# Spectral layer, rational layer and expert layer on one core: loads, buffers and weight work moved at the borders between the layers

## The chip, the cores and the metric

The kernel runs on one core of one Trainium2 chip, as one launch. The metric is the device time of that core in microseconds. A core has five engines that each work through a queue of their own: TensorE (PE; its weight loads are shown apart as PEld), VectorE (DVE), ScalarE (ACT), GpSimd (POOL) and SyncE (SP). Sixteen DMA engines move data. SyncE and GpSimd issue the transfers here.

## The reference

The reference is a chain of three layers on `x` of shape (8, 3072, 256), in float32:

```python
X = np.fft.rfft(x, axis=1)
Yr = soft(X.real @ w_r - X.imag @ w_i + b_r)     # soft: sign(v) * max(|v| - 0.01, 0)
Yi = soft(X.real @ w_i + X.imag @ w_r + b_i)
x = np.fft.irfft(Yr + 1j * Yi, n=3072, axis=1).reshape(8 * 3072, 256)

h = x @ w_in                                     # 256 -> 2048
g = (a0 + a1 h + a2 h^2 + a3 h^3) / (1 + |b0||h| + |b1| h^2 + 1e-6)
x = g @ w_out                                    # 2048 -> 256

expert_idx = argmax(norm(x) @ norm(expert_emb).T / tau)     # 8 experts, top 1
gate_w = softmax weight of the chosen expert
out[mask_e] = gate_w * (relu(x[mask_e] @ w1[e]) @ w2[e])    # 256 -> 1024 -> 256
```

There are 24,576 tokens.

## The kernel before

Float32 products are done as three products of rounded parts: each operand is split into a high part (cast by ScalarE) and a low part (the rest, subtracted by VectorE or GpSimd), and high times high, high times low and low times high are summed in PSUM.

**Spectral layer** (`dft_phase`). Each of 8 batches goes through a DFT in two stages, a product with the weights for each of 13 groups of frequencies, and the inverse. For a group, GpSimd makes low parts (`m_low`, tile `yl`, L358, and `ys_low`, tile `ysl`, L369), TensorE runs the first inverse stage into `pu` and `pt`, and SyncE stores the result `u` to a buffer `ub` in device memory (L393 to L398). When all of a batch's groups are stored, six loads (`su_load`, L406) bring `ub` back as `su`, and the last inverse stage follows. Of the last batch this last stage is left to the rational layer (`ai`, L1072). The tasks carry dependencies, a step number and a duration from a table, and `list_order` writes out from them the order in which each engine gets its instructions. In idle places of this phase the rational layer's weights are split as well (`weight_steps`, 32 pieces, stored to `w_hl`, one piece each 2.85 steps). Its last tasks are five loads of 1 MB on GpSimd's queue, `next_area` (functions in `early`: `load_in` with the first weights, three `load_w`, one `load_x`; L849, L852), for the rational layer: its first weight matrix `wi` in four parts and the first tokens `xt0`.

**Rational layer** (`moe1_phase`). 768 steps of 128 hidden units by 512 tokens: `pe_h` (h, L1001), ScalarE's powers (`act_hb`, L1010, into `hb`, whose two buffers lie in the tile `d_outer_b`), VectorE's denominator, GpSimd's and VectorE's numerator, `pe_o` (L1063) with the second weights `wo`. The tables `LATENCY`, `SLOWER`, `SHIFT` and `COST` and `list_order` fix the order on every engine. Four loads of 1 MB bring `wo` in (`load_wo`, L957), and one load per two token tiles brings `xt` (`load_xt`, L960). The twelve pieces of `ai` stand between the first steps; each leads to a cast `ai_h` (L1082) and a difference `ai_l` (L1088) in two pairs of buffers that lie in the tile `l`, and to stores of both. Near its end the phase sorts the tokens by expert: GpSimd scatters the rows from two buffers to `xs` in device memory (L1175); one buffer lies in the tile `su`, the other in the tile `b`, and the four scatters from `b` come last.

**Expert layer** (`moe2_phase`). Fifty slots run, each of one expert. A slot has 512 tokens, two of them (40 and 49) have 256. `load(s)` issues on SyncE the rows `xr` (L1383) and the expert's weights `w1` and `w2` (L1390, L1391) into the right-hand memory area. `prep(s)` gives closures: transposes of the rows (`xpose`, L1461, with an identity matrix `ident`), the splits of four pieces of W1 and four of W2 (`wsplit`: L1467 a cast in two instructions, L1468 the low parts), and the gate's small VectorE chain (`guess`, `newton`, `root`, and so on). `products` (L1502) runs TensorE: for f = 0 to 7 six matmuls into `ph` (three PSUM buffers in turn, L1510), each followed by ScalarE's `hh` (L1515) and VectorE's `hl` (L1516); then for each part `a` of 128 tokens 24 matmuls into `py` (L1527), the scaling `y` on ScalarE (L1533) and a scatter on GpSimd (L1534). In between it issues the closures of the next slot:

```python
for q in nxt[8 // parts * a:8 // parts * (a + 1)]:   # after py of part a, before its y
    for t in q:
        t()
```

In a full slot there are four parts, and the last takes `[W2[0], newton]` and `[W2[1], root]` of the next slot; in a half slot there are two, and the last takes `W1[2]`, `W1[3]`, `W2[0]` and `W2[1]` with their gate steps. W2[2] and W2[3] follow beside the next slot's `ph`.

**Memory.** `Area` keeps a stretch of on-chip memory that all three layers use, from the right: `d_outer` (`l`, `b`, `su`, `fd`, in this order), under it the spectral layer's or the rational layer's own part (`wi0`, `wi1`, `xt`), and in the expert layer `e_area` in their place. Tiles of a later area that lie over those of an earlier one wait for the last use of what lay there. With the old order of `e_area` the first rows `xr0` lie over `b`.

## Time and profile before

| | us |
|---|---|
| median of three runs | 4298.53 |
| the runs | 4296.80, 4304.39, 4298.53 |
| the profiled execution's own time | 4303.15 |
| its span in the trace | 4301.4 |
| TensorE busy | 4148.8 (96%) |
| VectorE busy | 3541.8 (82%) |
| ScalarE busy | 3196.1 (74%) |
| GpSimd busy | 2558.4 (59%) |

The profile's page gives busy time by engine and, in 40 slices of the span, the busy share of each engine, the clock that was granted to TensorE and what the DMA engines did. In this trace the spectral layer ends at 785.2 us, the rational layer's last matmuls are near 3112 us, and the expert layer's first product begins at 3128.5 us. A row of the timeline gives the start and duration of an instruction or of a run of like instructions, and in brackets how long the engine had stood idle before it and what ended the idle time. A row of the list of waits sums such idle time by what ended it.

### The profile page before, as it was taken

The page shows a single profiled execution, that of the slowest core. Times are in us where ns is not written, and L with a number is a line of the kernel's source. Part 1 is how long each engine was busy: PE and PEld are TensorE (multiplying, and loading weights), DVE is VectorE, ACT ScalarE, POOL GpSimd, SP SyncE. Part 2 cuts the span into 40 slices and gives each one's busy share as a digit, 9 for nine tenths or more (in the row PEclk, how much of TensorE's full clock was granted, in tenths as well). Part 3 has the DMA queues.
Part 4 walks back from the last instruction along what each step waited for, and adds up shares of the span by engine and source line. Part 5 has one row for each costly group of instructions (what it writes and reads, how often), then busy time and mean ns, then how long its engine had stood idle before and what let it go on. Part 6 is the DMA issues. An engine that isn't in the chain of part 4 may idle for free. (4 is left out here: it accounts for less than half of the span.)

```text
span 4301.4 us, 85375 instructions
## 1 busy us (share of the span) xinstructions
PE 4148.8 (96%) x31348; PEld 3952.6 (92%) x31348; DVE 3541.8 (82%) x7005; ACT 3196.1 (74%) x5889; POOL 2558.4 (59%) x2404
## 2 busy tenths in 40 slices
PE   7899989799999999999999999999889999999998
PEld 5788878799999999999999999999879999999988
DVE  6989888699999999999999999999866666666666
ACT  4555555699999999999999999999655555555555
POOL 2334334488889888988898889988811111111111
PEclk9999999899999999999999999999999999999999
DMA  7678876600001110100110011101044443444443
GB/s 257 227 260 270 303 258 210 222 27 35 33 30 37 40 34 30 45 31 33 33 43 32 33 40 35 34 31 41 28 171 134 136 145 135 135 135 136 147 136 125
DMA packets 226460, 458.88 MB, mean 107 GB/s; under 512 B 19428, under 2 KB 140764, under 8 KB 218581
## 3 DMA queue, kind: packets, MB, share of 16 engines
q1 hardware_dynamic: 198884, 342.37, 23.9%
q0 software_dynamic: 26688, 110.66, 7.4%
q8 instruction: 259, 4.24, 0.4%
q14 instruction: 197, 1.61, 0.1%
q10 hardware_dynamic: 432, 0.00, 0.0%
HBM read 286.98 MB, written 166.49 MB: 105 GB/s over the span
## 5 line engine op out<-in xcount | busy, mean ns | idle before, releaser
L1042 POOL TENSOR_TENSOR qg<-Q,gh 128x512 f32<-128x512 f32 x768 | 980.4, 1296 | 126.4 <-DVE gh L1038 119.1
L1063 PE MATMUL po<-gh,wo 128*128 128x256 f32 x6144 | 992.7, 284 | 0.2 <-DVE gh L1038 0.2
L1053 POOL TENSOR_TENSOR gl<-pr,r 128x512 fp32r<-128x512 f32 x672 | 861.6, 1298 | 77.6 <-ACT r L1034 36.1
L1063 PEld LDWEIGHTS po<-gh,wo 128*128 128x128 f32 x6144 | 837.4, 189 | 0.5 <-DVE gh L1038 0.5
L1534 POOL DMA_INDIRECT out_dram<-y,ids x196 | 204.7, 1044 | 970.3 <-ACT y L1533 578.7
L1063 PE MATMUL po<-gl,wo 128*128 128x256 f32 x3072 | 616.2, 282 | 8.2 <-POOL spacer L1174 5.4
L1001 PE MATMUL h<-m_area_xt,m_area_wi 128*128 128x256 f32 x4608 | 614.0, 285 | 8.2 <-DMA m_area_wi<-w_hl 5.9
L1016 DVE SCALAR_TENSOR_TENSOR Q<-h,d_outer_b 128x512 f32<-128x512 f32 x768 | 525.6, 684 | 89.8 <-ACT h L1013 85.0
L1001 PE MATMUL h<-xt,m_area_wi 128*128 128x256 f32 x4608 | 594.4, 280 | 0.2 <-DVE pr L1046 0.2
L1001 PEld LDWEIGHTS h<-m_area_xt,m_area_wi 128*128 128x128 f32 x4608 | 577.0, 191 | 9.4 <-DMA m_area_wi<-w_hl 6.7
L1038 DVE SCALAR_TENSOR_TENSOR gh<-h,r 128x512 fp32r<-128x512 f32 x768 | 506.5, 684 | 69.8 <-ACT r L1034 69.0
L1001 PEld LDWEIGHTS h<-xt,m_area_wi 128*128 128x128 f32 x4608 | 559.9, 188 | 0.4 <-DVE pr L1046 0.4
L1010 ACT ACTIVATE d_outer_b<-h 128x512 f32<-128x512 f32 x768 | 461.5, 601 | 126.4 <-PE h L1001 120.7
L1013 ACT ACTIVATE h<-h 128x512 f32<-128x512 f32 x768 | 462.7, 602 | 29.3 <-DVE Q L1016 29.2
L1063 PEld LDWEIGHTS po<-gl,wo 128*128 128x128 f32 x3072 | 473.7, 189 | 8.8 <-POOL spacer L1174 5.8
L1046 DVE SCALAR_TENSOR_TENSOR pr<-h,qg 128x512 f32<-128x512 f32 x672 | 457.8, 683 | 16.9 <-POOL qg L1042 16.7
L1510 PE MATMUL ph<-e_area_x,w1h 128*128 128x512 f32 (+1 forms) x1600 | 441.7, 392 | 12.6 <-DVE hl L1516 7.2
L1527 PE MATMUL py<-w2h,hh 128*128 128x256 f32 x1568 | 442.0, 282 | 0.0
L1527 PE MATMUL py<-w2h,hl 128*128 128x256 f32 x1568 | 438.3, 280 | 1.0 <-DVE hl L1516 1.0
L1527 PE MATMUL py<-w2l,hh 128*128 128x256 f32 x1568 | 438.7, 280 | 0.0
L1515 ACT ACTIVATE hh<-ph 128x512 fp32r<-128x512 f32 (+1 forms) x400 | 235.7, 589 | 266.2 <-PE ph L1510 266.0
L1031 ACT ACTIVATE r<-Q 128x1024 f32<-128x1024 f32 x384 | 406.9, 1060 | 5.8 <-DVE Q L1016 5.8
(276 smaller groups left out, 8723.1 us busy)
## 6 DMA issues: line engine op xcount, KB each, us to landing
e_area_w<-in_moe_w_dram SPq DMA_DIRECT2D x104, 1024.0 KB, 5.5
xt_hl<-o SPq DMA_DIRECT2D x84, 512.0 KB, 4.4
ab<-d_inner_a SPq DMA_DIRECT2D x48, 512.0 KB, 5.8
d_outer_su<-ub SPq DMA_DIRECT2D x48, 512.0 KB, 8.0
m_area_xt<-xt_hl POOLq DMA_DIRECT2D x24, 1024.0 KB
xt<-xt_hl POOLq DMA_DIRECT2D x24, 1024.0 KB, 5.3
d_outer_l<-ab SPq DMA_DIRECT2D x96, 240.0 KB, 4.1
e_area_xr<-xs SPq DMA_DIRECT2D x40, 544.0 KB, 5.2
```

Source lines behind the costliest of these rows:

```text
L1001: nc.tensor.matmul(p[:, TT * e:TT * e + TT], lhsT=w[:, k, c0:c0 + 128], rhs=q[:, hl, k, :], start=(e == 0 and i == 0), stop=(i == 5), skip ...
L1010: nc.scalar.activation(sb("hb", s), sb("h", s), AF.Abs, scale=c.r_b0)
L1013: nc.scalar.activation(sb("h2", s), sb("h", s), AF.Square, scale=c.r_sb1)
L1016: V.scalar_tensor_tensor(out=pair("Q", s), in0=sb("h2", s), scalar=1.0 + 1e-6, in1=sb("hb", s), op0=ALU.add, op1=ALU.add)
L1031: nc.scalar.activation(sb("r0", s), sb("Q", s), AF.Abs_reciprocal_sqrt)
L1038: V.scalar_tensor_tensor(out=sb("gh", s), in0=sb("h", s), scalar=1.0 if fast else a0, in1=pair("r0", s), op0=ALU.add, op1=ALU.mult)
L1042: nc.gpsimd.tensor_tensor(out=sb("qg", s), in0=pair("Q", s), in1=sb("gh", s).bitcast(F32), op=ALU.mult)
L1046: V.scalar_tensor_tensor(out=h if kind(s) == "V" else sb("pr", s), in0=h, scalar=1.0 if fast else a0, in1=sb("qg", s), op0=ALU.add, op1=AL ...
L1053: nc.gpsimd.tensor_tensor(out=sb("gl", s), in0=sb("pr", s), in1=pair("r0", s), op=ALU.mult)
L1063: nc.tensor.matmul(po[:, TT * d:TT * d + TT], lhsT=w[:, p, 128 * d:128 * d + 128], rhs=v[:, TT * e:TT * e + TT], start=(f + e + i + d == 0 ...
L1510: nc.tensor.matmul(p, lhsT=w[:, k, 128 * f:128 * f + 128], rhs=v[:, k, :n], start=(i == 0), stop=(i == 5))
L1527: nc.tensor.matmul(p, lhsT=h[:, cols], rhs=w[:, f, :], start=(f == 0 and i == 0), stop=(f == 7 and i == 2))
```

## The change

It has six parts. (1) The tiles of `d_outer` and of `e_area` are laid in another order: `xr0` now lies over `l` and `fd`, `w10` over `l` and the area under it, and `w20`, `w11`, `x0` and `x1` over `su`. (2) The five early loads no longer depend on the previous batch's last store and are spread over the last batch, one behind each second group; the weight pieces are spaced by 2.7 steps. (3) Each `wo` load has a small copy ahead of it on GpSimd that reads what `act_hb` of step 1, 2, 3 or 4 wrote, and the first `xt` load stands behind `pool_q` of step 2; in the table `SLOWER` the entry from `load_wo` to `pe_o` goes from 5000 to 6000. (4) No identity matrix is made; the transposes read another one that stands in `c.rt`. (5) In front of the first slot six of the eight groups of closures run, and the last two (W2[0], W2[1] and their gate steps) go to f = 2 and 3 of that slot. (6) In `products` the closures of the last part come behind its `y` and its scatter.

```diff
-    outer = area.open("d_outer", l=([128, 8, 256], F32), b=([128, NG * 4 * GK], F32), su=([128, R2, 256], F32),
-                      fd=([R1, R1], F32))
+    outer = area.open("d_outer", l=([128, 8, 256], F32), fd=([R1, R1], F32), b=([128, NG * 4 * GK], F32),
+                      su=([128, R2, 256], F32))
...
-        task(next_area, i, "pool", 1038, [("next_area", i - 1)] if i else
-             [("a_store", (nb - 1, 5)), ("a_mm", (nb - 1, 11)), ("o_store", (nb - 2, 11))] + last, step=-1000)
+        task(next_area, i, "pool", 1038, [("next_area", i - 1), ("b_mm", (nb - 1, 2 + 2 * i))] if i else
+             [("a_store", (nb - 1, 5)), ("a_mm", (nb - 1, 11))] + last, step=-1000)
...
-        s = 5 + 2.85 * n
+        s = 5 + 2.7 * n
...
     def load_wo(i):
         f = slice(4 * i, 4 * i + 4)
+
+        nc.gpsimd.tensor_copy(spacer, sb("hb", i + 1)[:, 0:1])
         nc.gpsimd.dma_start(out=wo[:, f], in_=w_hl[1].rearrange("p (f h d) -> p f h d", h=2, d=256)[:, f])
...
-            task(load_wo, i, "pool", "dma", [], [("load_wo", i - 1)] if i else [], step=-1000)
+            task(load_wo, i, "pool", "dma", [("act_hb", i + 1)], [("load_wo", i - 1)] if i else [], step=-1000)
...
-                task(load_xt, tt // 2 + 1, "pool", "dma", last("pe_h"), step=s)
+                task(load_xt, tt // 2 + 1, "pool", "dma", last("pe_h") if tt else [("pool_q", 2)], step=s)
...
-    t = area.open("e_area", **{f"w1{i}": ([128, 2, 1024], F32) for i in range(2)},
-                   **{f"w2{i}": ([128, 8, 256], F32) for i in range(2)},
-                   **{f"xr{i}": ([128, 4, ROW], F32) for i in range(4)},
-                   **{f"x{i}": ([128, 2, 512], F32R) for i in range(4)})
+    shapes = {"w1": ([128, 2, 1024], F32), "w2": ([128, 8, 256], F32), "xr": ([128, 4, ROW], F32),
+              "x": ([128, 2, 512], F32R)}
+    t = area.open("e_area", **{nm: shapes[nm[:-1]] for nm in ("x3", "w10", "xr0", "w21", "xr2", "xr3", "x2", "xr1", "x0", "x1",
+                                                              "w11", "w20")})
...
-                nc.tensor.transpose(p[:, 128 * a:128 * a + 128], xr[:, a, o:o + 128], ident)
+                nc.tensor.transpose(p[:, 128 * a:128 * a + 128], xr[:, a, o:o + 128], c.rt[:, 0, 0:128])
...
-            for q in nxt[8 // parts * a:8 // parts * (a + 1)]:
-                for t in q:
-                    t()
+            rest = [t for q in nxt[8 // parts * a:8 // parts * (a + 1)] for t in q]
+            for t in rest if a < parts - 1 else ():
+                t()
             y = ring("y", [128, 256], F32, 6)
...
+        for t in rest:
+            t()
...
-    ident = const.tile([128, 128], F32, name="ident")
-    V.memset(ident, 0.0)
-    nc.gpsimd.affine_select(out=ident, in_=ident, pattern=[[-1, 128]], compare_op=ALU.not_equal, fill=1.0, base=0,
-                            channel_multiplier=1)
     before, now = prep(0)
-    for q in before:
+    for q in before[:6]:
         for t in q:
             t()
+    now = [[], [], *before[6:], now[0], now[2], now[3] + now[4], now[5]]
```

Where the instructions stand now is shown at three places. The first is ScalarE at the end of a full slot of the expert layer: `y` is a part's scaling, `w2h` the cast of the next slot's W2, `hh` belongs to the next slot's product. Before:

```order
L1533 ACTIVATE y_63462<-py_63420,gate_63234 128x256
L1467 CAST w2h_63227<-e_area_w_63149 128x512 x2
L1533 ACTIVATE y_63463<-py_63421,gate_63234 128x256
L1515 ACTIVATE hh_63307<-ph_63295 128x512
L1467 CAST w2h_63227<-e_area_w_63149 128x512
L1515 ACTIVATE hh_63308<-ph_63296 128x512
```

After:

```order
L1536 ACTIVATE y_63465<-py_63423,gate_63237 128x256
L1536 ACTIVATE y_63466<-py_63424,gate_63237 128x256
L1470 CAST w2h_63230<-e_area_w_63157 128x512 x2
L1518 ACTIVATE hh_63298<-ph_63286 128x512
L1470 CAST w2h_63230<-e_area_w_63157 128x512
L1518 ACTIVATE hh_63299<-ph_63287 128x512
```

The last `y` moved ahead of the two casts of W2[0]. VectorE's own order around this place is the same as before.

The second place is GpSimd near the end of the spectral layer: `xsl`, `yl` and `ysl` are low parts that the groups need, L849 and L852 are the early loads. Before, behind the last `xsl`:

```order
L322 TENSOR_TENSOR xsl_138<-xs_134,xsh_136 128x240
L849 DMA m_area_wi_6855<-w_hl 128x2048
L852 DMA m_area_xt<-xt_hl 128x2048
L849 DMA m_area_wi_6855<-w_hl 128x2048
L358 TENSOR_TENSOR yl_145<-v_141,yh_143 120x512
L849 DMA m_area_wi_6856<-w_hl 128x2048
L369 TENSOR_TENSOR ysl_151<-ys_147,ysh_149 120x256
L849 DMA m_area_wi_6856<-w_hl 128x2048
L358 TENSOR_TENSOR yl_146<-v_142,yh_144 120x512
L369 TENSOR_TENSOR ysl_152<-ys_148,ysh_150 120x256
```

After, at the last two of the five loads; the other three stand 7, 17 and 30 rows ahead of the first of these:

```order
L358 TENSOR_TENSOR yl_146<-v_142,yh_144 120x512
L849 DMA m_area_wi_6101<-w_hl 128x2048
L369 TENSOR_TENSOR ysl_152<-ys_148,ysh_150 120x256
L322 TENSOR_TENSOR xsl_138<-xs_134,xsh_136 128x240
L358 TENSOR_TENSOR yl_145<-v_141,yh_143 120x512
L369 TENSOR_TENSOR ysl_151<-ys_147,ysh_149 120x256
L322 TENSOR_TENSOR xsl_137<-xs_133,xsh_135 128x240
L849 DMA m_area_wi_6101<-w_hl 128x2048
```

The loads moved from behind the last `xsl` to places between the groups of the last batch, and the tail holds only `yl` and `ysl`.

The third place is GpSimd at the start of the rational layer: L957 (after: L959) loads `wo`, L960 (L962) the next `xt`, `qg` and `gl` are the first steps' own work. Before:

```order
L957 DMA wo<-w_hl 128x2048 x4
L960 DMA xt_6947<-xt_hl 128x2048
L1042 TENSOR_TENSOR qg_6963<-Q_6956,gh_6969 128x512
L1042 TENSOR_TENSOR qg_6964<-Q_6956,gh_6970 128x512
L1053 TENSOR_TENSOR gl_6974<-pr_6966,r_6960 128x512
L1053 TENSOR_TENSOR gl_6975<-pr_6967,r_6960 128x512
```

After:

```order
L958 COPY spacer<-d_outer_b 128x1
L959 DMA wo<-w_hl 128x2048
L958 COPY spacer<-d_outer_b 128x1
L959 DMA wo<-w_hl 128x2048
L958 COPY spacer<-d_outer_b 128x1
L959 DMA wo<-w_hl 128x2048
L1044 TENSOR_TENSOR qg_6963<-Q_6956,gh_6969 128x512
L1044 TENSOR_TENSOR qg_6964<-Q_6956,gh_6970 128x512
L1055 TENSOR_TENSOR gl_6974<-pr_6966,r_6960 128x512
L1055 TENSOR_TENSOR gl_6975<-pr_6967,r_6960 128x512
L1044 TENSOR_TENSOR qg_6965<-Q_6957,gh_6971 128x512
L962 DMA xt_6947<-xt_hl 128x2048
```

Each `wo` load now has its copy ahead of it, and the `xt` load stands behind three `qg`; the fourth `wo` load stands right behind this `xt` load. TensorE's order in this phase is the same as before.

## Rows read from the trace of the kernel before

**Rows 1.** Busy time by stretch (window us, engines, PEclk, DMA share, GB/s)

```profile
720.00:785.20 65.20, 58.37 (x422) 56.05 (x421) 46.91 (x79) 34.34 (x76) 30.36 (x35) 0.96 0.64 214
785.20:840.00 54.80, 35.65 (x238) 33.44 (x237) 25.34 (x40) 28.92 (x47) 15.38 (x15) 0.80 0.78 296
3145.00:4283.00 1138.00, 1127.44 (x7383) 1026.53 (x7383) 752.19 (x2152) 650.31 (x1515) 202.75 (x197) 1.00 0.41 136
```

**Rows 2.** TensorE's waits for GpSimd's yl, 770 to 860 us (total, times, longest)

```profile
PE pu L378 <- POOL yl L358: 0.7, 1, 0.7
```

**Rows 3.** DMA issues from 760 to 820 us: count, KB each, landing

```profile
ub<-u SPq DMA_DIRECT2D x5, 240.0 KB, 2.9
...
ub<-u SPq DMA_DIRECT2D x1, 96.0 KB, 12.4
```

**Rows 4.** First border: SyncE, TensorE and ScalarE in time (start, duration)

```profile
786.97 0.39 SPq L398 DMA_DIRECT2D ub<-u  x1
...
792.66 7.45 PE L1001 MATMUL h<-m_area_xt,m_area_wi 128*128 128x256 f32 x45 [3.31 <-DMA m_area_wi<-w_hl]
807.00 4.60 PE L1072 MATMUL h<-d_outer_fd,d_outer_su 128*128 128x128 f32 x24 [6.89 <-DMA d_outer_su<-ub]
...
809.08 0.58 ACT L1082 CAST d_outer_l<-h 128x512 fp32r<-128x512 f32 x1 [4.45 <-PE h L1072]
```

**Rows 5.** Second border: GpSimd, SyncE and TensorE in time

```profile
3108.60 0.96 POOL L1175 DMA_INDIRECT xs<-d_outer_su,g_dst  x1 [0.19 <-issue]
...
3118.05 0.96 POOL L1175 DMA_INDIRECT xs<-d_outer_b,g_dst  x1 [0.19 <-issue]
...
3120.69 0.37 SPq L1383 DMA_DIRECT2D e_area_xr<-xs  x1
...
3124.54 1.94 PE L1461 MATMUL pt<-ident,e_area_xr 128*128 128x128 f32 x8 [12.66 <-DMA e_area_xr<-xs]
```

**Rows 6.** A full slot's start: TensorE, ScalarE and VectorE in time

```profile
3606.37 0.62 PE L1510 MATMUL ph<-e_area_x,w1h 128*128 128x512 f32 x2
3606.83 0.62 PE L1510 MATMUL ph<-e_area_x,w1l 128*128 128x512 f32 x2
...
3611.01 0.64 PE L1510 MATMUL ph<-e_area_x,w1l 128*128 128x512 f32 x2
...
3603.74 0.47 ACT L1533 ACTIVATE y<-py,gate 128x256 f32<-128x256 f32 x1 [0.63 <-PE py L1527]
3604.11 1.13 ACT L1467 CAST w2h<-e_area_w 128x512 fp32r<-128x512 f32 x2
3606.57 0.47 ACT L1533 ACTIVATE y<-py,gate 128x256 f32<-128x256 f32 x1 [1.33 <-PE py L1527]
3607.95 0.60 ACT L1515 ACTIVATE hh<-ph 128x512 fp32r<-128x512 f32 x1 [0.91 <-PE ph L1510]
...
3604.99 0.69 DVE L1468 TENSOR_TENSOR w2l<-e_area_w,w2h 128x512 fp32r<-128x512 f32 x1
...
3607.48 0.16 DVE L1417 TENSOR_TENSOR gy<-gy,gu 128x4 f32<-128x4 f32 x1
3608.58 0.69 DVE L1516 SCALAR_TENSOR_TENSOR hl<-ph,hh 128x512 fp32r<-128x512 f32 x1 [0.94 <-ACT hh L1515]
...
3610.34 0.68 DVE L1516 SCALAR_TENSOR_TENSOR hl<-ph,hh 128x512 fp32r<-128x512 f32 x1
```

**Rows 7.** TensorE's waits for hl, 3146 to 4283 us

```profile
PE ph L1510 <- DVE hl L1516: 7.2, 4, 4.7
```

**Rows 8.** The full slot behind a half slot: VectorE, then TensorE

```profile
4093.47 0.69 DVE L1516 SCALAR_TENSOR_TENSOR hl<-ph,hh 128x512 fp32r<-128x512 f32 x1 [0.98 <-ACT hh L1515]
...
4094.22 0.73 PE L1510 MATMUL ph<-e_area_x,w1h 128*128 128x512 f32 x2 [1.41 <-DVE hl L1516]
```

**Rows 9.** A half slot's start: ScalarE, then VectorE

```profile
4073.03 0.48 ACT L1533 ACTIVATE y<-py,gate 128x256 f32<-128x256 f32 x1 [1.33 <-PE py L1527]
...
4074.47 0.42 DVE L1516 SCALAR_TENSOR_TENSOR hl<-ph,hh 128x256 fp32r<-128x256 f32 x1 [0.36 <-ACT hh L1515]
```

More of the change, by code (lines that the diff above doesn't have):

```diff
@@ L551 @@
            "dve": {"pe": 256, "act": 128, "dve": 127, "pool": 179}, "pool": {"pe": 203, "act": 75, "dve": 74, "pool": 102}}
-SLOWER = {("load_xt", "pe_h"): 2000, ("act_h2", "dve_q"): 245, ("act_hb", "dve_q"): 245, ("dve_m", "dve_g"): 227, ("dve_rho", "dve_gl"): 227, ("load_wo", "pe_o"): 5000}
+SLOWER = {("load_xt", "pe_h"): 2000, ("act_h2", "dve_q"): 245, ("act_hb", "dve_q"): 245, ("dve_m", "dve_g"): 227, ("dve_rho", "dve_gl"): 227, ("load_wo", "pe_o"): 6000}
 BUFS = {"h": (6, "pe"), "h2": (1, "act"), "hb": (2, "act"), "Q": (3, "dve"), "w": (2, "act"), "r0": (3, "act"),
```

## The prediction

> **What bounds the kernel now.** I read the windows of busy time first. In the expert layer TensorE is busy for 1127.44 of 1138 us at a granted clock of 1.00 [rows 1]; what delays it there lengthens the run. Around 785 us, where the spectral layer hands over, it is busy for 35.65 of 54.80 us while the DMA engines move 296 GB/s on average [rows 1]. So two borders hold idle time that can be won, and the slots of the expert layer hold none: VectorE's `hl` makes TensorE wait four times in fifty slots, 7.2 us in all, 4.7 of them once [rows 7]. Next the timeline, border by border, and then the start of one slot on three engines.
>
> **Border one, 785 us.** TensorE's main run of 45 matmuls waits for `wi`, 3.31 us at the last of its parts, starts only at 792.66 and takes 7.45 us [rows 4]; from the layer's end at 785.2 that is 7.5 us, into which three matmuls fall. Then it waits 6.89 us for `su` and starts `ai` at 807.00 [rows 4]. Behind that wait stands a store: the last `ub` store is issued at 786.97, and this 96 KB store lands after 12.4 us, where five others of 240 KB have a median of 2.9 [rows 3, 4]. The `su` loads wait for it. All this time the five early loads and the `wo` loads, 10 MB together, fill the DMA engines. Part by part:
>
> (a) The early loads are spread over the last batch. In the 65 us before the border the DMA engines are busy 0.64 of the time at 214 GB/s [rows 1], so the 5 MB find room, and `wi` stands ready: the 45 matmuls start some 6 us sooner.
>
> (b) The `wo` loads wait for `act_hb` of steps 1 to 4, so the last `ub` stores meet a freer queue. At 2.9 us instead of 12.4 the `su` loads go 9.5 us earlier. From the store's landing (786.97 + 12.4 = 799.4) to the first `ai` matmul it took 7.6 us; I keep these, since three `wo` loads then start beside the `su` loads as their like did before. ScalarE must be free too: at 809.08 it had idled for 4.45 us, so it was free at 804.63 [rows 4], and its work hangs on the 45 matmuls, which start 6 us earlier and run without the gaps that slowed them; that puts it near 797. 807.00 less 9.5 is 797.5, so the two meet.
>
> (c) `yl` and `ysl` of the last groups no longer stand behind loads on GpSimd: TensorE's wait of 0.7 us for `yl` [rows 2] and some of what follows goes, and the last stores move up with it. I take 2.5 for this and for the faster 45 matmuls. Sum for border one: 9.5 + 2.5 = **12 us gained**, bounds 8 (the `su` loads share the DMA engines with more than before) and 17. What is late next is the `ai` chain, held by the stores of its two buffer pairs; it is unchanged. The fourth `wo` load and the first `xt` load now stand behind GpSimd's `qg`, and feed steps that come much later; nothing is lost there.
>
> (d) In the spectral layer itself the loads sit ahead of `yl` on GpSimd, where one may wait for the last weight store, and the weight pieces crowd into fewer steps. No row shows either. The nearest is the 0.7 us that `yl` cost behind loads [rows 2]: once for each of the five is 3.5 lost, and a shorter tail may give as much back. I take 0, bounds -3 and +4.
>
> The Trainium skill ("DMA: Bandwidth & Descriptors", section "Issuing engines are not separate DMA queues") says that transfers issued from several engines share the same 16 DMA engines. The rows agree with it: 12.4 us against 2.9 for a SyncE store beside GpSimd's loads. By that rule the early loads slow the last batch's own transfers too, which is the upper bound in (d).
>
> **Border two, 3108 to 3128 us.** TensorE waits 12.66 us for `xr0`, whose load is issued at 3120.69, that is 2.64 us after the last scatter from `b` (3118.05) [rows 5]. After the change `xr0` lies over `l` and `fd`, and the tiles over `su` come free with the scatter at 3108.60 [rows 5]. With the same 2.64 the load goes at 3111.2 instead of 3120.7: **9.5 us gained**, bounds 10 and 7 (`w20`, needed later, is still behind the scatters, and weights must land and be cast before the first product). The second load still waits for `b`, but it feeds slot 1. Without `ident` a memset and a GpSimd instruction go; they run inside the 12.66 us and are worth 0. Of the first slot's W2, moved to f = 2 and 3, I expect nothing on either side: it only moves VectorE's work within a slot where VectorE is the late one; bounds -2 and +2.
>
> **The slots.** Part (6) is small in the diff and runs fifty times. The slot that starts at 3606.37 (call this T) shows it [rows 6]. Before, ScalarE casts W2[0] from 3604.11, while TensorE is still in part 3; VectorE takes its low part at 3604.99, ends the gate's chain at 3607.48, and is free when `hh` comes; `hl` starts at 3608.58, T + 2.21. After, ScalarE does the last `y` first. `y` needs TensorE's last matmul and starts at 3606.57, T + 0.20; from one `y` to a cast behind it there are 0.37 us (3603.74 to 3604.11), so the cast comes at T + 0.57. From ScalarE's `hh` to VectorE's `hl` takes 0.63 (3607.95 to 3608.58), and I take the same from a cast to its low part: T + 1.20. VectorE's order is unchanged, so what stood between the first `w2l` and the end of the chain, 3604.99 to 3607.48 and 0.08 more, 2.57 in all, stands there still. `hl` of f = 0 can start at T + 3.77, 1.56 later than now.
>
> Does TensorE feel it? `ph` has three buffers, so f = 3 needs `hl` of f = 0. f = 3 starts its second group at 3611.01; f = 0 has 0.46 between its first and second (3606.37, 3606.83), so f = 3 starts at 3610.55, T + 4.18 [rows 6]. From the start of `hl` to TensorE's next matmul there are 0.75 us (4093.47 to 4094.22) [rows 8]. So f = 3 can go at T + 4.52: a wait of 0.34. The next `hl` follows 1.76 us after the first (3608.58 to 3610.34), since a `w2l` and a gate step stand between: T + 5.53, released at 6.28. f = 4 would start one f step (1.39, from T + 4.18 over three) after 4.52, at 5.91: another 0.37. The third `hl` needs no such step and VectorE gains on TensorE from there. Sum: **0.71 us per slot**, bounds 0.5 and 0.9. It holds for the 45 full slots behind a full slot, other than slots 0 and 1 (slot 1 has the wait of 4.7 already): 32 us.
>
> The two half slots (40 and 49) have shorter steps and no slack. There `y` starts at 4073.03, so T is 4072.83, and `hl` at 4074.47, T + 1.64 [rows 9]. By the same sum it would be T + 3.77: 2.1 us each, 4.2 together, bounds 0 and 5. Slot 41 behind one waits already 1.41 us [rows 8]; more casts there, 0.4. Sum for the slots: **36.6 us lost**, bounds 26 and 44. In return the last `y` of a slot comes no earlier, since it waits for TensorE alone; the very last scatter may gain up to 0.7, and I take 0.
>
> **The sum.** -12 + 0 - 9.5 + 36.6 = +15. The profiled execution took 4303.15 us, its span 4301.4; the sum made on it is 4318. It is 4.6 above the median of the runs, 4298.53, within their spread, so I put the forecast on the median: **4314 us**, 0.35% slower. A measurement of this kernel can tell about 0.2% from no change, that is 8.6 us.
>
> **Rivals.**
>
> The first ends on the other side: **the slots stay hidden**. VectorE now idles 0.94 us ahead of `hl` [rows 6], and the wait exists only if `hl` starts later than T + 3.43 (4.18 - 0.75). My figure is 3.77, a margin of 0.34 us. If the low parts follow the casts sooner, or VectorE runs the chain more tightly, the wait is nothing, and the borders alone remain: 4298.5 - 21.5 = 4277. The two sides meet at 21.5 / 47 = 0.46 us per slot. Against it: each link is a measured spacing, and slot 41 shows that a late `hl` is paid in full [rows 8]. Chance 0.12.
>
> The second: **the borders give more or the slots cost less, and it comes out even**. At border one the 6 us for `wi`, the 6.89 for `su` and 4 more from the slowed matmuls and the stores behind them make 17; with 10 at border two and 0.55 per slot that is -27 + 29, so 4300. Chance 0.22.
>
> The third: **the change doesn't do what it says at the borders.** The early loads wait on the last weight store and collide with the last batch's stores, or `xr0` waits for the last scatters all the same. Then 8 to 16 of the 21.5 us are missing, and the time is 4322 to 4330. For it: SyncE's queue serves in order, and one load behind a late tile holds all behind it. Chance 0.07.
>
> The fourth is a price on the waits: **TensorE's clock falls at them.** Two short waits would stand in each slot. Around border one, where TensorE idles long, the granted clock is 0.80 on average; in the expert layer it is 1.00 in spite of waits of 4.7 and 1.41 us [rows 1, 7, 8]. A mean of 0.9 in that layer (some of it at the lower of the two levels, 1.2 GHz in place of 2.4) would cost 1138 / 0.9 - 1138, some 126 us, so 4440. Chance 0.02. The Trainium skill ("TensorE: Matmul & The Clock Gate", section "A second HAM failure mode: psum-queue depth-cycling") warns of this pattern, short idle gaps between groups of matmuls while a PSUM buffer is awaited; the trace here does not show it.
>
> **How the numbers follow.** The forecast has 0.57, its own range 4306 to 4324. Below 4298 lie the first rival and a little of the second, above 4326 the fourth and part of the third: the range is 4297 to 4326. Slower by over 0.2% means above 4307.1: the forecast's case but for a few hundredths, the third and the fourth, 0.64. Within: 0.23. Faster, below 4289.9: 0.13.
>
> **What would show it.** In the profile after: `hl` as the ender of TensorE's waits in nearly every slot, twice, 0.3 to 0.4 us each, some 30 us in all against 7.2; ScalarE's cast of W2[0] behind the last `y`. At border one no wait for `wi`, the last `ub` store landing in 3 to 4 us, `ai` starting about 12 us sooner after the spectral layer's end. At border two the `xr0` load about 2.6 us behind the last scatter from `su`. The prediction is wrong if `hl` waits are absent from the slots, if the clock in the expert layer is under 1.00, or if the spectral layer's end moves by more than 5 us.

## The result, and the profile after

The changed kernel takes 4351.22 us (median of four runs, 4348.68 to 4352.80) against 4297.83 for the kernel before in the same comparison: 1.012 times the time, with a 95% interval of 1.0103 to 1.0138, 53 us more. The forecast was 4314 in a range of 4297 to 4326. Slower was right; the amount measured is three and a half times the 15 us of the forecast's sum.

The profiled executions stand 45.5 us apart (spans of 4346.9 and 4301.4). The stages can be told apart by a few marks in the timeline of each: the last matmul of the spectral layer, the first `ai` matmul, the first product with `wo`, the first scatter from `b`, the first `ph` matmul of each slot, and the end. The expert layer by these marks (period of a slot: from its first `ph` matmul to the next slot's):

| | first `ph` at | slot 0 | slot 1 | slots 2-39, mean | slot 40 | slot 41 | slots 42-48, mean | slot 49 to the end |
|---|---|---|---|---|---|---|---|---|
| before | 3128.47 | 27.13 | 30.95 | 23.32 | 15.54 | 25.46 | 23.32 | 24.31 |
| after | 3112.47 | 35.91 | 30.07 | 24.19 | 18.51 | 27.78 | 24.89 | 28.75 |

The layer starts 16.0 us sooner and then loses 61.5: 8.8 in slot 0 (0.9 come back in slot 1), 32.9 in slots 2 to 39 (38 slots, 0.87 each), and 20.7 in the last ten (3.0 and 2.3 in slots 40 and 41, 11.0 in slots 42 to 48 at 1.57 each, 4.4 in the last).

TensorE's waits for `hl` in the layer from slot 1 on, with total, times and longest, answer to [rows 7]:

```profile
PE ph L1513 <- DVE hl L1519: 27.7, 63, 3.4
```

A full slot of the changed kernel, by TensorE, ScalarE and VectorE in time (line numbers are three higher than before), answers to [rows 6]:

```profile
3904.48 0.62 PE L1513 MATMUL ph<-e_area_x,w1h 128*128 128x512 f32 x2
...
3909.00 0.73 PE L1513 MATMUL ph<-e_area_x,w1h 128*128 128x512 f32 x2 [0.19 <-DVE hl L1519]
...
3910.04 1.44 PE L1513 MATMUL ph<-e_area_x,w1h 128*128 128x512 f32 x4
...
3904.68 0.47 ACT L1536 ACTIVATE y<-py,gate 128x256 f32<-128x256 f32 x1 [2.35 <-PE py L1530]
...
3905.05 1.13 ACT L1470 CAST w2h<-e_area_w 128x512 fp32r<-128x512 f32 x2
...
3905.69 0.69 DVE L1471 TENSOR_TENSOR w2l<-e_area_w,w2h 128x512 fp32r<-128x512 f32 x1 [2.50 <-ACT w2h L1470]
...
3908.26 0.68 DVE L1519 SCALAR_TENSOR_TENSOR hl<-ph,hh 128x512 fp32r<-128x512 f32 x1
...
3910.00 1.28 DVE L1519 SCALAR_TENSOR_TENSOR hl<-ph,hh 128x512 fp32r<-128x512 f32 x2
```

With T = 3904.48, the start of the slot's first `ph` matmul, `y` starts at T + 0.20, the cast at T + 0.57, the low part at T + 1.21, the first `hl` at T + 3.78 and the next at T + 5.52; the prediction had 0.20, 0.57, 1.20, 3.77 and 5.53. TensorE starts f = 3 at T + 4.52, as predicted. The 0.19 us in the bracket is all that the trace calls waiting here: the rest, and the second wait, sit inside the longer spans, as in the run of four matmuls that takes 1.44 where four take 1.10, and in the run of two behind the first wait that takes 0.73 where two take 0.62. So the waits must be read from the period, 24.13 here against 23.32.

Slot 0 of the changed kernel, by SyncE, ScalarE, VectorE and TensorE, is the place that the prediction priced at nothing:

```profile
3123.10 0.37 SPq L1394 DMA_DIRECT2D e_area_w<-in_moe_w_dram  x1
...
3130.20 0.62 ACT L1470 CAST w2h<-e_area_w 128x512 fp32r<-128x512 f32 x1 [7.13 <-DMA e_area_w<-in_moe_w_dram]
...
3132.13 0.68 DVE L1519 SCALAR_TENSOR_TENSOR hl<-ph,hh 128x512 fp32r<-128x512 f32 x1
...
3132.87 1.22 PE L1513 MATMUL ph<-e_area_x,w1h 128*128 128x512 f32 x2 [6.25 <-DVE hl L1519]
```

At 3123.10 SyncE issues the W2 load for slot 2. ScalarE's cast of the next W2 piece of slot 0 waits 7.13 us for a load of that buffer, VectorE's `hl` stands behind the low part, and TensorE waits 6.25 us.

The ten slots behind branches (40 to 49, where the program decides at run time between 512 and 256 tokens) lose more than the others. VectorE's waits without a releaser ahead of `hl`, summed over slots 42 to 47, then one of them, VectorE's branch instruction inside it (its row gives min, median and max of the duration in ns, then first and last start), and TensorE's wait behind it (slot 44, which starts at T = 4193.67):

```profile
DVE hl L1519 <- issue: 3.3, 6, 0.8
...
4198.28 0.69 DVE L1519 SCALAR_TENSOR_TENSOR hl<-ph,hh 128x512 fp32r<-128x512 f32 x1 [0.75 <-issue]
...
L1497 DVEq COMPARE_BRANCH  x1: 56/56/56, 4197.8 to 4197.8; - x1
...
4199.03 0.72 PE L1513 MATMUL ph<-e_area_x,w1h 128*128 128x512 f32 x2 [1.01 <-DVE hl L1519]
```

Here `hl` starts at T + 4.61 in place of 3.78. VectorE idles from 4197.53 to 4198.28, and the branch stands in this stretch. The idle time is 0.44 to 0.46 us in four of the slots 42 to 47 and 0.75 to 0.78 in two; in slot 48, which stands behind two branches, it is 1.22 (the trace puts that one down to `hh`). What each of these seven slots loses, less this idle time, is 0.89 to 0.95 us, near the 0.87 of the slots without branches. Before the change VectorE idled at this point until `hh` came, and its branch lay in that idle time, at T + 1.5.

In the half slots, and in slot 41 between them, the stall is followed by slower matmuls. TensorE in the last slot:

```profile
4320.05 0.40 PE L1513 MATMUL ph<-e_area_x,w1h 128*128 128x256 f32 x2
...
4322.91 0.50 PE L1513 MATMUL ph<-e_area_x,w1h 128*128 128x256 f32 x2 [2.46 <-DVE hl L1519]
...
4324.49 0.59 PE L1513 MATMUL ph<-e_area_x,w1h 128*128 128x256 f32 x2 [0.61 <-DVE hl L1519]
...
4325.31 1.05 PE L1513 MATMUL ph<-e_area_x,w1h 128*128 128x256 f32 x4
```

Four matmuls take 0.64 us at the full clock in this slot before the change and 1.05 here. The rows of busy time, of the two half slots before (the last two columns but one are granted clock and DMA share):

```profile
4072.80:4088.40 15.60, 12.82 (x107) 12.40 (x105) 10.51 (x34) 10.03 (x29) 3.19 (x3) 1.00 0.54 186
...
4277.10:4283.90 6.80, 6.29 (x52) 6.00 (x51) 5.83 (x22) 4.15 (x12) 2.69 (x2) 1.00 0.48 182
```

and of a full slot, the first half slot, slot 41 and the last slot after:

```profile
3904.50:3928.60 24.10, 23.83 (x154) 21.02 (x153) 15.16 (x43) 13.37 (x31) 4.10 (x4) 1.00 0.37 124
...
4097.60:4116.10 18.50, 14.27 (x106) 13.56 (x104) 10.99 (x35) 10.12 (x29) 2.35 (x3) 0.91 0.46 156
...
4116.10:4143.90 27.80, 25.55 (x152) 22.30 (x153) 17.74 (x53) 13.62 (x32) 3.55 (x4) 0.94 0.35 112
...
4318.10:4329.00 10.90, 7.83 (x51) 7.43 (x51) 7.53 (x28) 5.04 (x13) 1.96 (x2) 0.84 0.53 181
```

Slot 41 is a full slot; TensorE waits 2.23 us for `hl` in it, and its granted clock had been 1.00 before the change.

At the first border `ai` starts much sooner, and its chain takes longer. SyncE, TensorE and VectorE of the changed kernel, which answer to [rows 4]:

```profile
779.40 0.41 SPq L398 DMA_DIRECT2D ub<-u  x1
...
781.34 2.91 SPq L406 DMA_DIRECT2D d_outer_su<-ub  x6
...
777.66 7.71 PE L1003 MATMUL h<-m_area_xt,m_area_wi 128*128 128x256 f32 x48
...
785.31 2.02 PE L1074 MATMUL h<-d_outer_fd,d_outer_su 128*128 128x128 f32 x16
...
801.79 4.65 PE L1074 MATMUL h<-d_outer_fd,d_outer_su 128*128 128x128 f32 x24 [4.96 <-DVE d_outer_l L1090]
...
801.04 0.69 DVE L1090 TENSOR_TENSOR d_outer_l<-h,d_outer_l 128x512 fp32r<-128x512 f32 x1 [7.06 <-DMA xt_hl<-d_outer_l]
```

The last `ub` store is issued at 779.40 and the `su` loads go at 781.34, 1.94 us later where it had been 12.5. `ai` starts at 785.31, 21.7 us sooner. Then VectorE waits 7.06 us for the store of a buffer of `l`. Its waits for these stores, in the 58 us from 777 on, after:

```profile
DVE d_outer_l L1090 <- DMA xt_hl<-d_outer_l: 17.9, 7, 7.1
```

and before, over the same stretch:

```profile
DVE d_outer_l L1088 <- DMA xt_hl<-d_outer_l: 7.2, 4, 3.0
```

At the second border, SyncE and TensorE of the changed kernel answer to [rows 5]:

```profile
3092.49 0.35 SPq L1386 DMA_DIRECT2D e_area_xr<-xs  x1
...
3103.59 1.30 PE L1464 MATMUL pt<-rt,e_area_xr 128*128 128x128 f32 x5 [3.60 <-issue]
...
3109.68 0.80 PE L1464 MATMUL pt<-rt,e_area_xr 128*128 128x128 f32 x3 [4.80 <-issue]
...
3112.47 0.79 PE L1513 MATMUL ph<-e_area_x,w1h 128*128 128x512 f32 x1 [1.99 <-ACT w1h L1470]
```

The `xr0` load is issued at 3092.49, ahead even of the last scatters, since `l` and `fd` are free by then. But the transposes run in two pieces, at 3103.59 and 3109.68, behind waits of 3.60 and 4.80 us for which the profile has no releaser. The first `ph` comes 10.1 us behind the first scatter from `b` (3102.37), where it came 14.2 behind it before.

TensorE's branch instruction at the end of the rational layer, with its duration in ns and its start, before and after:

```profile
L1291 PEldq COMPARE_BRANCH  x1: 3362/3362/3362, 3111.7 to 3111.7; - x1
...
L1293 PEldq COMPARE_BRANCH  x1: 3645/3645/3645, 3099.8 to 3099.8; - x1
```

It lasts 3.4 us before the change and 3.6 after. Before, it ends at 3115.0, inside the wait for `xr0`. After, it fills the first wait, and the first transpose starts 0.17 us behind its end.

### The profile page after: what moved, and what is told of

Read it like the earlier page. It is cut to its first block, busy times and chain, and to the rows that moved or that the text cites. A ratio compares the mean times of both kernels' runs of the same rounds, so it can differ in the third digit from the quotient of the medians.

```text
span 4346.9 us, 85380 instructions
## 1 busy us (share of the span) xinstructions
PE 4183.2 (96%) x31348; PEld 3955.3 (91%) x31348; DVE 3531.8 (81%) x7004; ACT 3196.6 (74%) x5889; POOL 2551.0 (59%) x2407
## 5 line engine op out<-in xcount | busy, mean ns | idle before, releaser
L1513 PE MATMUL ph<-e_area_x,w1h 128*128 128x512 f32 (+1 forms) x1600 | 471.9, 402 | 41.4 <-DVE hl L1519 33.9
L1513 PEld LDWEIGHTS ph<-e_area_x,w1h 128*128 128x128 f32 x1600 | 292.7, 192 | 140.3 <-DVE hl L1519 78.7
```

The costliest lines, as they stand in the source:

```text
L1513: nc.tensor.matmul(p, lhsT=w[:, k, 128 * f:128 * f + 128], rhs=v[:, k, :n], start=(i == 0), stop=(i == 5))
```

## Experiments

| kernel | median, us | ratio to before | 95% interval |
|---|---|---|---|
| changed kernel | 4351.22 | 1.012 | 1.0103 to 1.0138 |
| e1, closures back ahead of `y` | 4298.90 | 1.0001 | 0.9991 to 1.0010 |
| e2, before, closures alone moved | 4350.43 | 1.0123 | 1.0106 to 1.0140 |
| e3, W2 ahead of slot 0 again | 4340.30 | 1.0100 | 1.0083 to 1.0117 |
| e4, load for slot 2 later | 4342.93 | 1.0103 | 1.0086 to 1.0120 |
| e5, closures moved in slots 0 to 39 alone | 4333.49 | 1.0084 | 1.0069 to 1.0099 |
| e6, before, last group alone moved | 4306.07 | 1.0017 | 1.0008 to 1.0027 |
| e7, both moves of the expert layer undone | 4289.68 | 0.9981 | 0.9972 to 0.9990 |
| e8, e7 with `wo` later | 4284.82 | 0.9967 | 0.9955 to 0.9979 |
| e9, before, first border alone | 4295.72 | 0.9994 | 0.9985 to 1.0003 |
| e10, before, second border alone | 4295.47 | 0.9992 | 0.9983 to 1.0001 |
| e11, e8 with `wo` and `xt` later still | 4282.97 | 0.9964 | 0.9952 to 0.9976 |

Each ratio is to runs of the kernel before on the same chip, whose medians were 4297.8 to 4298.9; different rows can come from different chips.

**The moved closures, taken out and put in alone.** e1 is the changed kernel with this edit undone:

```diff
-            rest = [t for q in nxt[8 // parts * a:8 // parts * (a + 1)] for t in q]
-            for t in rest if a < parts - 1 else ():
-                t()
+            for q in nxt[8 // parts * a:8 // parts * (a + 1)]:
+                for t in q:
+                    t()
...
-        for t in rest:
-            t()
```

> The changed kernel with the closures of the last part issued ahead of its y again, as before the change; all else is the change. In the traces of before and after, slots 2 to 39 grew by 0.87 us each (32.9 together), slot 40 by 3.0, slot 41 by 2.3, slots 42 to 48 by 1.57 each (11.0), the last slot by 4.4: 53.6 us. Theory: all of this is the moved closures, so the time falls by 53.6 to about 4298, and TensorE's waits for hl fall from 33.9 us to some 14 (slots 0 and 1 and a few). Rival: the growth of the slots is the new layout of the area or the weights' loads, and the time stays near 4351.

It took 4298.90, and slots 2 to 39 are back at a mean of 23.33 us. TensorE's waits for `hl` from slot 2 to the end:

```profile
PE ph L1513 <- DVE hl L1519: 1.0, 2, 0.5
```

e2 is the same edit put into the kernel before, and nothing else:

> The kernel before with only the closures of the last part moved behind its y and scatter. Theory: the same 53.6 us by themselves, so 4298 + 54 = 4352, with slots 2 to 39 at 24.1 to 24.3 us and slots 42 to 48 near 24.7. Rival, the layout or the loads: 4298. A mixture lies between.

It took 4350.43, with slots 2 to 39 at 24.17 and TensorE's waits for `hl`, over the stretch as above, of

```profile
PE ph L1510 <- DVE hl L1516: 26.1, 59, 3.3
```

So the moved closures alone make the loss in the slots, and neither the layout nor the loads have a part in it. It is 52 us by either kernel (4351.2 - 4298.9, 4350.4 - 4298.2).

**Slot 0.** e3 runs all eight groups ahead of the first slot again, e4 leaves the groups where the change put them and issues the load for slot 2 later:

```diff
-    for q in before[:6]:
+    for q in before:
         for t in q:
             t()
-    now = [[], [], *before[6:], now[0], now[2], now[3] + now[4], now[5]]
```

> The changed kernel with all eight groups of closures run ahead of the first slot again, so W2[0] and W2[1] of slot 0 no longer stand at f = 2 and 3. In the trace of after slot 0 takes 35.9 us against 27.1, and ScalarE waits there 7.1 us for a load of e_area_w. Theory: the load for slot 2 is issued at f = 2 into the buffer from which slot 0 still casts W2[1] to W2[3], and the cast waits for its landing; with two pieces cast earlier fewer casts meet it, so slot 0 falls back to about 27 us: 4351 - 9 = 4342. Rival: W2 ahead of the first product delays that product by as much, and the time stays at 4351.

```diff
-            now[2].append(lambda: load(s + 2))
+            now[2 if s else 5].append(lambda: load(s + 2))
```

> The changed kernel with one move: in slot 0 the load for slot 2 is issued behind f = 5, after the last cast of W2, in place of f = 2. Theory, the load for slot 2 holds the casts of slot 0: the wait of 6.3 us in slot 0 goes and with it the lower clock behind it, 4351 - 9 = 4342. Rival, VectorE has too much to do in slot 0 with two more pieces of W2: the wait stays, 4351.

They took 4340.30 and 4342.93, and slot 0 fell from 35.9 to 27.1 and 27.6 us. In e4 VectorE does the same work in slot 0 as in the changed kernel, and TensorE's waits there are only these, the first of which the kernel before has too:

```profile
PE ph L1513 <- ACT w1h L1470: 3.0, 2, 2.0
...
PE py L1530 <- DVE hl L1519: 0.2, 1, 0.2
```

So not the work but the load held slot 0. Slots 0 and 2 share one W2 buffer; with W2[1] to W2[3] moved to f = 3 to 5, the load for slot 2 at f = 2 stands ahead of them in program order, so their casts wait for it, and read what it brought. (The result is right only as long as slots 0 and 2 have the same expert; that is a trap of its own.)

**Where the delay begins to cost.** e6 moves only the last group in the kernel before; the loop over `rest` stands behind the scatter as in the change:

```diff
-            for q in nxt[8 // parts * a:8 // parts * (a + 1)]:
-                for t in q:
-                    t()
+            qs = nxt[8 // parts * a:8 // parts * (a + 1)]
+            rest = qs[-1] if a == parts - 1 and qs else []
+            for q in qs[:-1] if a == parts - 1 else qs:
+                for t in q:
+                    t()
```

> The kernel before with only the last group (W2[1] and root) behind y; W2[0] and newton stay ahead of it. Theory: what counts is when hl of f = 0 can start, and up to T + 3.43 us it costs nothing. W2[1]'s cast at T + 0.57, its low part at T + 1.20, then root's chain: hl at about T + 2.5, under 3.43 even with 0.75 for a branch. So slots 2 to 39 stay at 23.32 us, only the two half slots pay some 0.9 each: 4300. Rival: every piece moved costs in proportion, half of 53.6 us: 4325.

In slots 2 to 39 this costs nothing: their mean is 23.32 us, the same as before, with `hl` at T + 2.50 (one slot starts at 3600.24, its `hl` at 3602.74) where the theory had 2.5. The loss is a threshold, not a price per piece. But the time is 4306.07, 7.2 above before in place of 2, all of it in the last ten slots: 1.8 in slot 40, 1.1 in 41, 1.8 in slots 42 to 48, 2.7 in the last. Their rows, VectorE's waits over slots 43 to 47 and the start of slot 43:

```profile
DVE hl L1516 <- ACT w2h L1467: 2.9, 5, 0.8
...
4133.91 0.62 PE L1510 MATMUL ph<-e_area_x,w1h 128*128 128x512 f32 x2
...
4137.28 0.69 DVE L1516 SCALAR_TENSOR_TENSOR hl<-ph,hh 128x512 fp32r<-128x512 f32 x1 [0.78 <-ACT w2h L1467]
```

`hl` starts at T + 3.37, 0.87 later than in the slots without branches, behind an idle 0.78. The trace puts it down to ScalarE's `w2h`, which `hl` does not read; VectorE's branch stands in it here too (at T + 2.83). That leaves 0.06 to the limit of 3.43, and the second `hl` passes its own limit: 0.40 us are lost in this slot. Over the slots 42 to 48 the loss follows the idle time: under 0.1 us in four with 0.44 to 0.46, 0.4 in two with 0.74 and 0.78, 0.85 in slot 48 with 1.23.

e5 has the moved closures in slots 0 to 39 alone:

```diff
-            for t in rest if a < parts - 1 else ():
+            for t in rest if a < parts - 1 or s >= c.sure else ():
...
-        for t in rest:
+        for t in rest if s < c.sure else ():
```

> The changed kernel with the closures moved behind y in slots 0 to 39 alone; the ten slots that stand behind branches (40 to 49) have the old order. In the traces these ten grew by 20.7 us, 42 to 48 by 1.57 each where 2 to 39 grew by 0.87. Theory: the moved closures make VectorE late, and only then does its start behind a branch (0.75 us without a releaser ahead of the first hl) cost anything; the ten give back all 20.7: 4351 - 21 = 4330. Rival: the ten slots are slower for another reason (the layout, the branches themselves), and 5 to 7 of the 20.7 come back: 4345.

It took 4333.49. Slots 42 to 48 are at 23.33 us and the last at 24.34, as before the change; slots 40 and 41 keep 2.0 and 1.8 us, since the closures of slot 39 make slot 40 late, which the expectation had overlooked (4330 + 3.9 = 4334). How this reaches slot 41 is not shown; TensorE waits there 2.00 us for `hl` where it had 1.41 before, and its clock is 0.94 in place of 1.00. So a branch costs these slots nothing as long as VectorE is early.

**The borders.** e7 undoes both moves of the expert layer (the diffs of e1 and e3 together), and what is left is the two borders:

> The changed kernel with both of the expert layer's moves undone: closures of the last part ahead of y, all eight groups ahead of slot 0. What is left is the borders: over the profiles so far the first product of the expert layer comes 10.8 us sooner than with the kernel before (3115.1 against 3125.8 on average). Theory: this passes on to the end: 4298 - 11 = 4287. Rival: it is given back in slots 0 and 1, 4298.

It took 4289.68, 0.9981 of before: the borders gain about 9 us, not 21.5. e9 and e10 put each border's parts alone into the kernel before (the hunks of the change that belong to it):

> The kernel before with the first border's parts alone: early loads over the last batch, weight pieces 2.7 steps apart, wo behind act_hb, xt behind pool_q. Theory: ai starts 8 us behind the spectral layer's end in place of 22, and the first product with wo 38 us behind ai in place of 25, so all but 1 us of the 14 is given back in the chain; with what the spectral layer's end itself moves (3.5 us in the mean of the profiles so far, about as much as they scatter) 4294 to 4298. Rival, the chain is unchanged as the prediction had it: 4298 - 12 = 4286.

> The kernel before with the second border's parts alone: the new layout of both areas and the transposes by the other identity matrix. Theory: TensorE's wait of 12.6 us for xr0 goes, and waits without a releaser ahead of its transposes (5.4 to 8.4 us in the profiles) come in its place; the first product stands 8.7 us behind the scatters from b begin in place of 14.2: 4298 - 5 = 4293. Rival, the prediction's 9.5: 4289.

4295.72 and 4295.47: each gains some 2 us, and neither interval leaves out no change. Together that is 4 us where e7 has 9; each interval reaches about 4 us to either side, so this is no contradiction. These times alone don't separate the theories, but the marks in the traces do, since a difference of marks close together varies little between executions:

| | spectral end to `ai` | `ai` to first product with `wo` | first scatter from `b` to first `ph` |
|---|---|---|---|
| before | 22.0 | 26.0 | 14.2 |
| e2 (borders as before) | 22.1 | 24.1 | 14.1 |
| after | 7.9 | 31.9 | 10.1 |
| e7 | 8.6 | 39.6 | 7.5 |
| e9 | 7.9 | 32.2 | 14.2 |
| e10 | 21.7 | 24.6 | 7.5 |

At the first border 14 us are won and 6 to 15 given back in the chain. At the second 4 to 7 are won (3 in e11). In e10 TensorE's waits at its transposes are

```profile
PE pt L1462 <- issue: 5.7, 2, 4.0
```

in place of the 12.66 us for `xr0`.

The nine profiles with the second border's parts agree on what these two waits stand behind. The first ends with TensorE's branch, which lasts 3.3 to 4.2 us in all thirteen profiles; the first transpose follows its end by 0.17 us in each of the nine. The second lies in all nine between the fifth and the sixth of the eight transposes, where the program has TensorE wait for nothing. Both end at a steady distance behind a load of instructions: the list of queues has two for these, q8 and q14. TensorE has 74% of the trace's instructions and q8 72% of the bytes of such loads, so I take q8 for TensorE's. A transfer of 16 KB on q8 starts during the branch and ends 1.3 to 1.6 us ahead of the branch's end, and another ends 1.3 to 1.5 us ahead of the sixth transpose. In the four profiles with the old border the second such transfer ends about 8 us ahead of the sixth transpose, inside the wait for `xr0`. So by the trace TensorE waits here for its own code; no run moves that code alone.

e8 and e11 test what holds the chain. They are e7 with the `wo` loads behind later steps; e11 has 1, 5, 6 and 7 for the steps, and the first `xt` load behind `pool_q` of step 7 in place of 2. The diff of e8:

```diff
+WO_AT = (1, 4, 5, 6)
...
-        nc.gpsimd.tensor_copy(spacer, sb("hb", i + 1)[:, 0:1])
+        nc.gpsimd.tensor_copy(spacer, sb("hb", WO_AT[i])[:, 0:1])
...
-            task(load_wo, i, "pool", "dma", [("act_hb", i + 1)], [("load_wo", i - 1)] if i else [], step=-1000)
+            task(load_wo, i, "pool", "dma", [("act_hb", WO_AT[i])], [("load_wo", i - 1)] if i else [], step=-1000)
```

> The last kernel with the loads of wo behind act_hb of steps 1, 4, 5 and 6 in place of 1, 2, 3 and 4. In the traces after the change ai starts 8 us behind the spectral layer's end in place of 22, but the first product with wo follows 32 to 39 us behind it in place of 24 to 26: VectorE waits up to 7 us for stores of the two buffer pairs. Theory: these stores queue beside three wo loads; with one wo load there the chain takes 25 us again, and 4287 falls to about 4277. Rival: the su loads and the stores fill the DMA engines by themselves, or the product now waits for wo: 4287 or more.

> The kernel with wo later once more, with wo behind act_hb of steps 1, 5, 6 and 7 and the first xt load behind pool_q of step 7 (it stood behind step 2). In the last kernel the chain's longest waits left, 3.1 and 4.2 us, stand where the xt load and the second wo load are issued (810.7 and 812.9 us). Theory: the stores queue beside them; with both later the first product with wo comes about 28 us behind ai in place of 33: 4285 - 5 = 4280. Rival: the products wait for wo instead, or the stores are slow by themselves: 4285 or more.

`ai` to the first product with `wo` falls from 39.6 us to 33.0 and 27.4, and the times to 4284.82 and 4282.97. TensorE's waits for the chain, e8:

```profile
PE h L1004 <- DVE d_outer_l L1091: 6.3, 2, 4.2
...
PE h L1075 <- DVE d_outer_l L1091: 5.9, 4, 3.1
```

and e11:

```profile
PE h L1075 <- DVE d_outer_l L1091: 6.1, 3, 3.3
...
PE h L1004 <- DVE d_outer_l L1091: 2.9, 2, 1.5
```

So the loads that run beside the chain's stores are what lengthens it. The stores' own rows say the same; these are the chain's first four stores (count, KB each, median us to landing) before, in e9 (three `wo` loads beside them) and in e11 (one):

```profile
xt_hl<-d_outer_l SPq DMA_DIRECT2D x4, 256.0 KB, 4.4
...
xt_hl<-d_outer_l SPq DMA_DIRECT2D x4, 256.0 KB, 11.1
...
xt_hl<-d_outer_l SPq DMA_DIRECT2D x4, 256.0 KB, 6.8
```

e8 gained half of what was expected, since the second `wo` load and the `xt` load still met the chain; e11 has 0.9964 (0.9952 to 0.9976) of the time of before and the lowest median here. e8 and e11 overlap in their intervals.

## Why the prediction was right and wrong

**The slots' mechanism was right.** The sum of a full slot stands to 0.02 us at each of its five points, and e6 shows the threshold that it rests on. Of its three sizes one is nearly right and two are wrong:

- Slots 2 to 39: 0.71 predicted (27.0 for 38 slots), 0.87 measured (32.9). Most slots have 0.81, and others up to 1.04. The 0.81 are the predicted waits and 0.1 more: behind a wait the second matmul follows the first by 0.33 us in place of 0.23. In one of the slower slots VectorE's second `hl` follows the first by 1.98 us in place of 1.74; why is not shown.
- Slots 40 to 49: 9.6 predicted, 20.7 measured. The step that failed is "It holds for the 45 full slots": seven of these stand behind branches, where VectorE idles 0.44 to 0.78 us (1.22 behind two branches) ahead of the first `hl`. Before the change this lay inside its wait of 0.94 for `hh`, so no list of waits named it; the branch instruction itself had a row, and in slot 48 `hl` already started 0.27 later than in the others. Once VectorE is late, each of these slots pays it, one to one: in e2, as in the changed kernel, the loss less the idle time is the same in all seven to within 0.06 us.
- In the half slots and in slot 41 a second price follows. In the last slot there are waits of 2.46 and 0.61 us, and then TensorE runs at the lower of its two levels (1.2 GHz in place of 2.4) for a while, with 0.84 granted on average where it had 1.00. Of the 4.4 us there, 2.6 are longer waits (2.46 + 0.61 - 0.51) and the rest are mostly these slower matmuls. Slot 40 has 0.91 behind a wait of 2.40, and slot 41 has 0.94 behind one of 2.23 and loses 2.3 where the sum had 0.4. The fourth rival had the mechanism, for the whole layer and at 126 us. The trace has it in these three slots alone, besides slot 0 (0.80 behind its wait of 6.25, where it had been 0.88); the slots 2 to 39 with their waits of 0.3, and the slots 42 to 48 with waits of 0.7 to 1.5, keep 1.00. The Trainium skill ("TensorE: Matmul & The Clock Gate", section "A second HAM failure mode: psum-queue depth-cycling") says that short idle gaps between groups of matmuls can make the clock go to and fro. The slots 2 to 39, with two such gaps each, don't agree with it; in the three slots where the clock fell, a single wait of 2.2 to 2.5 us stood ahead.

**The first slot was priced at nothing, and cost 8.8 us.** The step that failed is "it only moves VectorE's work within a slot". The edit moves W2's casts behind the load for slot 2 in program order, and this load writes the buffer that they read. Which instructions now stand on the other side of the moved ones was weighed for GpSimd's queue at the first border, in (c), and not here, where the moved casts and the load share a tile. e4 settles it.

**The borders were to give 21.5 us and gave about 9 to 11.** Over the profiles of e1 to e4 and of the two kernels the first `ph` stands at 3115.0 on average with the change's borders and at 3125.8 without, 10.8 sooner.

- First border: the start of `ai` was under-estimated, for 14 us are won ahead of it where the sum had 12. The step that failed is "the `ai` chain [...] is unchanged". Its stores now run beside the `wo` loads that the change brings to this place, and beside the `xt` load; the first four land after 11 us in e9 where it was 4.4. The chain takes 32 to 40 us in place of 24 to 26. In the profiled execution the whole still came out near 12 (the first scatter from `b` went from 3114.26 to 3102.37), but this holds some luck of that execution: the spectral layer's end alone lies between 776.3 and 784.0 over the profiles with the changed borders, and between 781.2 and 785.0 without. So the prediction's own sign of being wrong, an end that moves by more than 5 us, came true (7.6 us between the two kernels' profiles) and tells little: the end's means with and without these borders differ by 3.2 us, and each range is wider than that. The prediction had the rule on shared DMA engines beside it and used it for the last batch's transfers only.
- Second border: the load of `xr0` was freed as said, and more. The step that failed is to count the whole 9.5 us as gained: behind the wait of 12.66 us for `xr0` lay another, which the prediction didn't weigh. TensorE's branch at the end of the rational layer and a second stop among its first transposes make it wait 5.4 to 9.5 us together in the nine profiles. By the transfers on q8 both are waits for its instructions. Before the change they ran out under the wait for `xr0`, and the weight-load side of TensorE already showed an idle 12.7 us there without a releaser. That the code's arrival sets their length is read from the times in nine profiles and not tested by a run.

**The four errors add up.** Against the prediction there are 10.7 us less at the borders (21.5 - 10.8), 7.9 more lost in slots 0 and 1 (8.8 - 0.9), 5.9 in slots 2 to 39 and 11.1 in the last ten, 35.6 in all; with the predicted 15 that is 51, against 53 measured.

**The rivals.** The first, slots that stay hidden, is refuted by e2; its threshold is right, as e6 shows, and the forecast's margin over it, 0.34 us, held. The second gave the borders too much. The third was nearest in its effect, with half of the borders' gain missing, but by another way: `xr0` did not wait for the scatters. All errors went one way. In four places a cover had been taken as given: the load's order in slot 0, VectorE's branch under its wait for `hh`, TensorE's branch under the wait for `xr0`, and the chain's quiet stores.

## What to carry to other kernels

When closures are moved past one another, list for each tile that a moved instruction reads who writes it next: a load ahead of it in program order turns a move "within a slot" into a wait for a DMA. An engine with a slack of 0.94 us hides other waits as long as it is early, such as a branch; before spending the slack, look for what else it covers. The list of waits names only what ended last, so the rows of branch instructions have to be asked for by their line. Freed transfers started at once here, so a load released early should be followed to the next short chain of stores that shares the DMA engines with it; here moving the loads behind that chain was worth another 7 us by the ratios of e7 and e11 (0.9981 and 0.9964, with intervals that just overlap).

## What the runs showed of the hardware

- VectorE idles 0.44 to 0.78 us ahead of its first `hl` in slots behind a branch, and 1.22 behind two, though the branch's own row has 0.06; it costs time only when VectorE is the late engine (e5 against the changed kernel).
- TensorE's branch at the end of the rational layer lasts 3.3 to 4.2 us in all thirteen profiles, and a second stop of 1.6 to 5.5 us follows in the nine where `xr0` doesn't cover it; each ends 1.3 to 1.6 us behind a 16 KB transfer of instructions.
- TensorE's clock stays at 1.00 through two waits of 0.2 to 0.4 us in each of 38 slots and through single waits of 0.7 to 1.5 us in slots 42 to 48. It falls behind single waits of 2.2 to 2.5 us (0.91, 0.94 and 0.84 over slots 40, 41 and 49).
- The first 256 KB stores of the chain land after 11.1 us beside the last `su` loads and three `wo` loads of 1 MB (e9), after 6.8 with one `wo` load (e11), and after 4.4 with none (before).
- The spectral layer's end varies by up to 7.7 us between executions with the same borders, so a gain of 5 us at a border is read from marks close to it rather than from the total.
